# Value buffers as parts of one tile, wq in two transfers of three and two rows, and V of head 1 loaded ahead of K of head 2

## The chip, the cores and the metric

The kernel runs on one core of one Trainium2 chip. The metric is the device time of one execution in microseconds (us). A run more than 1.5% above the fastest of its kernel counts as slow.

The engines are PE (matrix products), DVE (vector), ACT (scalar), POOL, and SP, the sync engine, which in this kernel does nothing but issue loads. Sixteen DMA engines move the data. A load is issued once and is split over all sixteen. It has landed when the last of them is done. SP issues in program order: when the next load in its program has to wait for a buffer, every load behind it waits too. I call the loads that SP has issued and that haven't moved yet the **queue**.

## The reference, cut to what matters

```python
def reference(A_x, A_k_cache, A_v_cache, A_wq, A_wo, B_x, B_w1, B_w3, B_w2):
    # A_x [4, 1, 640]; caches [4, 32, 8192, 192]; wq [640, 6144]; all bf16
    xn = layernorm(A_x)
    q = (xn @ A_wq) as [4, 32 heads, 1, 192]
    k, v = the last W = 2048 rows of the caches
    p = softmax(einsum("bhqd,bhkd->bhqk", q, k) * 192 ** -0.5)
    attn = einsum("bhqk,bhkd->bhqd", p, v) as [4, 1, 6144] @ A_wo
    ffn = (silu(xn @ B_w1) * (xn @ B_w3)) @ B_w2          # F = 1536
    return A_x + attn + ffn
```

One decoding step reads 32 K tiles and 32 V tiles of 3.15 MB each (128 partitions of 24,576 B), wq of 7.86 MB, and smaller weights: 223 MB in all, for little arithmetic.

## The kernel before

All large loads go through the sync queue. K has two buffers and V has three. The query weights wq lie in the V buffers until the query projection has read them, so V of head 0 can't be loaded before that.

```python
kpool = tc.tile_pool(name="kt", bufs=KBUFS)      # KBUFS = 2
vpool = tc.tile_pool(name="vt", bufs=VBUFS)      # VBUFS = 3

def load_v(h):
    vt = (vpool if h < H - 1 else kpool).tile([P, NJ, Dh], BF16, ...)
    nc.sync.dma_start(out=vt..., in_=v_win[:, h]...)
    vts[h] = vt
# load_k(h) is the same with kpool and k_win
...
x_sb = const.tile([B, D], BF16, name="x_sb")
nc.scalar.dma_start(out=x_sb[:], in_=A_x...)     # x on ACT's queue
for k0 in range(0, KC, 2):                       # wq: 2 + 2 + 1 rows per partition
    n = min(2, KC - k0)
    wt = vpool.tile([P, 2, H * Dh], BF16, tag="vt")
    nc.sync.dma_start(out=wt[:, 0:n, :]..., in_=wq_v[:, k0:k0 + n, :]...)
for h in range(KBUFS):
    load_k(h)                                    # K of heads 0 and 1
...
xf = ppool.tile([B, D], FP32, tag="pr")
nc.vector.tensor_copy(out=xf[:], in_=x_sb[:])    # the x cast: start of LN, q projection, all heads
```

Each head is cut into four units u of a quarter tile. A unit has one DVE multiply of K by the query, an adder on PE (six matmuls that sum over the head dimension), and a DVE reduction. Four multiplies free a K buffer. Work is put into slots. A slot is emitted by phase, and this order is also the order on each engine.

```python
def mult(u):
    h, g = u // GQ, u % GQ                       # GQ = 4
    pr = ppool.tile([P, JQ, Dh], BF16, tag="pr")
    nc.vector.tensor_tensor(out=pr[:], in0=kts[h][:, g * JQ:(g + 1) * JQ, :], in1=<q of head h>, op=ALU.mult)
...
for h in range(H):
    u0, ul = h * GQ, h * GQ + GQ - 1
    if h >= KBUFS:
        add(*early.get(h, ((h - KBUFS + 1) * GQ, 0)), load_k, h)   # K(h): slot 4(h-1), waits for the multiplies on K(h-2)
    if h < H - 2:
        add(u0 + 2, 0, load_v, h)                                  # V(h): slot 4h+2
    for u in range(u0, ul + 1):
        add(u, 1, mult, u)
        add(u + 1, 2, adder, u)
        add(u + 1, 8, reduce_quarter, u)
...
add(3, 0, w1_load)                                                 # FFN weights in between
```

I write K2 for "K of head 2", and so on. In the sync queue the order is K0, K1, V0, w1, K2, V1, K3, V2, K4, V3 and so on. K2 waits until K0 has been multiplied, K4 until K2 has been multiplied.

## Time and profile before

| | before |
|---|---|
| median of 6 runs | 525.96 us (525.79 to 527.08) |
| span of the profiled execution (it took 525.93 us) | 524.1 us |
| bytes moved | 223.26 MB |

These lines are from the first parts of the profile page of the kernel before. The row "DMA" gives the busy tenths of the sixteen DMA engines in 40 equal slices of the span, the row "GB/s" what they moved. q1 is the queue of the large loads, q8 the queue on which instructions are fetched. The last line gives the shares of the chain of waits that ended last.

```profile
span 524.1 us, 4775 instructions
...
DMA  9999999999999999999999999999999999999996
GB/s 391 422 441 413 437 427 432 428 435 439 425 435 430 440 428 431 429 430 439 427 432 431 435 427 435 433 431 431 430 435 430 435 428 433 437 424 438 428 427 263
DMA packets 11138, 223.26 MB, mean 426 GB/s; under 512 B 1246, under 2 KB 1366, under 8 KB 1622
...
q1 hardware_dynamic: 11102, 222.96, 99.2%
q8 instruction: 15, 0.25, 0.2%
...
DMA 60%; DVE 19%; PE 18%; ACT 2%; issue 1%; SPq 0%
```

The DMA engines are at nine tenths or more in 39 of 40 slices. In stretches of 100 us and in one of 80, from 100 to 480 us, the window table gives 431 or 432 GB/s, and in stretches of 20 us 430 to 434. The Trainium skill ("DMA: Bandwidth & Descriptors", Where 436 GB/s comes from) works out a ceiling of 435.2 GB/s for the ports into the core's memory. This trace agrees: those long stretches lie within 1% of it. The same section says that for transfers between HBM, where the caches lie, and that memory a lower limit of about 358 GB/s binds. These loads come from HBM and run at 431 GB/s, so here the measurement decides. So the kernel is bound by DMA, and its time is the bytes divided by the rate, plus the moments at which an engine has no bytes to move.

The sync-queue timeline of the kernel before shows when loads were issued. Columns: start in us, length in us, SP's sequencer, source line, operation, destination and source, count.

```profile
25.96 0.54 SPq L134 DMA_DIRECT2D vt<-in_A_v_cache_dram  x1
...
40.58 0.54 SPq L128 DMA_DIRECT2D kt<-in_A_k_cache_dram  x1
...
42.19 0.57 SPq L134 DMA_DIRECT2D vt<-in_A_v_cache_dram  x1
51.86 0.54 SPq L128 DMA_DIRECT2D kt<-in_A_k_cache_dram  x1
...
65.00 0.54 SPq L128 DMA_DIRECT2D kt<-in_A_k_cache_dram  x1
65.63 0.55 SPq L134 DMA_DIRECT2D vt<-in_A_v_cache_dram  x1
```

The lines are V0, K2, V1, K3, K4 and V3. K2 was issued at 40.58, V1 right behind it, and K4 at 65.00.

The DVE timeline of the kernel before has the x cast and the first multiply on K2. The bracket gives DVE's idle time before it and what ended that.

```profile
6.89 0.48 DVE L180 CAST xf<-x_sb 4x640 f32<-4x640 bf16 x1 [4.01 <-DMA x_sb<-in_A_x_dram]
...
55.06 1.76 DVE L283 TENSOR_TENSOR pr<-kt,qbc 128x3072 bf16<-128x3072 bf16 x1 [2.63 <-DMA kt<-in_A_k_cache_dram]
```

x landed by 6.89 us, and K2 by 55.06 us. K4 was issued 65.00 - 55.06 = 9.9 us later, when K2's four multiplies were done.

### The profile page before, as it was taken

The page shows a single profiled execution, that of the slowest core. Times are in us where ns is not written, and L with a number is a line of the kernel's source. Part 1 is how long each engine was busy: PE and PEld are TensorE (multiplying, and loading weights), DVE is VectorE, ACT ScalarE, POOL GpSimd, SP SyncE. Part 2 cuts the span into 40 slices and gives each one's busy share as a digit, 9 for nine tenths or more (in the row PEclk, how much of TensorE's full clock was granted, in tenths as well). Part 3 has the DMA queues.
Part 4 walks back from the last instruction along what each step waited for, and adds up shares of the span by engine and source line. Part 5 has one row for each costly group of instructions (what it writes and reads, how often), then busy time and mean ns, then how long its engine had stood idle before and what let it go on. Part 6 is the DMA issues. An engine that isn't in the chain of part 4 may idle for free.

```text
span 524.1 us, 4775 instructions
## 1 busy us (share of the span) xinstructions
PE 356.9 (68%) x2327; PEld 75.5 (14%) x1633; DVE 339.3 (65%) x398; ACT 55.9 (11%) x176; POOL 5.4 (1%) x11
## 2 busy tenths in 40 slices
PE   0965867574685786863867676765776876685786
PEld 0100111110111111110111121111111111111122
DVE  3278756485676767763667876573776867666851
ACT  2111112000011101110110011100011110011020
POOL 4000000000000000000000000000000000000000
PEclk9989887977889988897898899888798898889898
DMA  9999999999999999999999999999999999999996
GB/s 391 422 441 413 437 427 432 428 435 439 425 435 430 440 428 431 429 430 439 427 432 431 435 427 435 433 431 431 430 435 430 435 428 433 437 424 438 428 427 263
DMA packets 11138, 223.26 MB, mean 426 GB/s; under 512 B 1246, under 2 KB 1366, under 8 KB 1622
## 3 DMA queue, kind: packets, MB, share of 16 engines
q1 hardware_dynamic: 11102, 222.96, 99.2%
q8 instruction: 15, 0.25, 0.2%
q14 instruction: 5, 0.04, 0.0%
q10 hardware_dynamic: 16, 0.01, 0.0%
HBM read 222.96 MB, written 0.01 MB: 425 GB/s over the span
## 4 chain that ended last, share of the span: by engine, by line
DMA 60%; DVE 19%; PE 18%; ACT 2%; issue 1%; SPq 0%
DMA kt<-in_A_k_cache_dram 52%; DVE pr L283 13%; PE ps L294 9%; DMA w<-in_B_w_dram 7%; PE po L367 3%; PE qps L248 3%; DVE sc L302 3%; DVE z L338 1%; DMA x_sb<-in_A_x_dram 1%; ACT ex L330 1%; PE acc L269 1%; PE mt L324 1%; ACT L330 0%; PE mt L311 0%; ACT negm L327 0%
## 5 line engine op out<-in xcount | busy, mean ns | idle before, releaser
L294 PE MATMUL ps<-pr,idb 128*128 128x512 bf16 x768 | 212.2, 418 | 145.9 <-DVE pr L283 145.8
L283 DVE TENSOR_TENSOR pr<-kt,qbc 128x3072 bf16<-128x3072 bf16 x128 | 223.5, 1747 | 106.6 <-DMA kt<-in_A_k_cache_dram 106.6
L302 DVE TENSOR_REDUCE sc<-ps 128x16 f32<-128x512 f32 x128 | 87.1, 681 | 1.5 <-PE ps L294 1.5
L346 PE MATMUL o_ps<-vt,z 128*8 128x384 bf16 x1024 | 55.5, 361 | 0.8 <-DMA vt<-in_A_v_cache_dram 0.8
L367 PE MATMUL po<-o_sb,sel_w 128*32 128x192 f32 x128 | 48.5, 513 | 1.1 <-ACT o_sb L349 1.1
L346 PEld LDWEIGHTS <-z 128*8 128x8 bf16 x1024 | 24.9, 92 | 101.4 <-issue 91.4
L338 DVE TENSOR_TENSOR z<-ex,mask_b 128x256 bf16<-128x256 bf16 x32 | 13.6, 425 | 34.1 <-ACT ex L330 34.0
L349 ACT COPY o_sb<-o_ps 128x384 f32<-128x384 f32 x32 | 15.3, 479 | 189.4 <-PE o_ps L346 189.4
L319 ACT ACTIVATE gneg<-gmax 1x128 f32<-1x128 f32 x32 | 9.8, 308 | 174.2 <-DVE gmax L316 174.2
L311 PEld LDWEIGHTS mt<-idf,lmax 128*1 128x1 f32 x32 | 3.3, 102 | 138.2 <-issue 138.2
L367 PEld LDWEIGHTS po<-o_sb,sel_w 128*32 128x32 f32 x128 | 14.2, 131 | 28.2 <-issue 24.7
L294 PEld LDWEIGHTS <-idb 128*128 128x128 bf16 x123 | 11.8, 96 | 37.4 <-issue 30.8
L324 PEld LDWEIGHTS mt<-ones_ff,gneg 1*128 1x128 f32 x64 | 9.4, 182 | 46.4 <-issue 39.2
L248 PE MATMUL qps<-wt,xnT 128*128 128x512 bf16 x59 | 14.7, 407 | 0.1
L316 DVE TENSOR_REDUCE gmax<-mt 1x4 f32<-1x128 f32 x32 | 8.8, 274 | 6.6 <-PE mt L311 6.5
L324 PE MATMUL mt<-ones_ff,gneg 1*128 1x1 f32 x64 | 12.1, 256 | 0.7 <-ACT gneg L319 0.7
L327 ACT COPY negm<-mt 128x1 f32<-128x1 f32 x32 | 5.1, 159 | 68.6 <-PE mt L324 68.6
L354 PEld LDWEIGHTS po<-rsum,tot_w 128*32 128x32 f32 x64 | 4.5, 108 | 49.3 <-ACT ex L330 35.3
L330 ACT ACTIVATE ex<-sc,negm 128x64 bf16<-128x64 f32 x32 | 11.1, 347 | 1.0
L254 DVE CAST qbc<-qps 128x512 bf16<-128x512 f32 x6 | 3.8, 685 | 11.5 <-PE qps L248 11.5
L311 PE MATMUL mt<-idf,lmax 128*1 128x128 f32 x32 | 11.1, 346 | 0.0
L202 PE MATMUL xnT_ps<-idb,xn 4*128 4x4 bf16 x5 | 0.4, 178 | 13.5 <-DVE xn L197 13.5
(73 smaller groups left out, 81.5 us busy)
## 6 DMA issues: line engine op xcount, KB each, us to landing
kt<-in_A_k_cache_dram SPq DMA_DIRECT2D x32, 3072.0 KB, 18.6
vt<-in_A_v_cache_dram SPq DMA_DIRECT2D x32, 3072.0 KB, 25.4
wt<-in_A_wq_dram SPq DMA_DIRECT2D x2, 3072.0 KB, 9.7
wo_t<-in_A_wo_dram SPq DMA_DIRECT2D x3, 1920.0 KB, 23.3
w<-in_B_w_dram SPq DMA_DIRECT2D x2, 1920.0 KB, 27.0
wt<-in_A_wq_dram SPq DMA_DIRECT2D x1, 1536.0 KB, 19.5
w<-in_B_w_dram SPq DMA_DIRECT2D x1, 1536.0 KB, 19.8
wo_t<-in_A_wo_dram SPq DMA_DIRECT2D x1, 1120.0 KB
```

The costliest lines, as they stand in the source:

```text
L248: nc.tensor.matmul(qp[:], lhsT=xnT[:, kc].rearrange("p a b -> p (a b)"), rhs=wq_rows[kc][:, (c0 + i) * QC:(c0 + i + 1) * QC], start=(kc == ...
L283: nc.vector.tensor_tensor(out=pr[:], in0=kts[h][:, g * JQ:(g + 1) * JQ, :], in1=qbc[:, h * Dh:(h + 1) * Dh].unsqueeze(1).to_broadcast([P, ...
L294: nc.tensor.matmul(ps[:], lhsT=idb[:], rhs=pr[:, :, kk * DD:(kk + 1) * DD], start=(kk == 0), stop=(kk == NK - 1))
L302: nc.vector.tensor_reduce(out=scs[h][:, g * JQ:(g + 1) * JQ], in_=pss.pop(u)[:], axis=AX.X, op=ALU.add)
L311: nc.tensor.transpose(out=mt[0:1, 0:P], in_=chs[h][0][:], identity=idf[:])
L319: nc.scalar.activation(out=gneg[:], in_=gmax[:].unsqueeze(1).to_broadcast([1, PB, B]), func=ACTF.Copy, scale=-SCALE)
L324: nc.tensor.matmul(mt[:, P:P + 1], lhsT=gneg[:].rearrange("o p b -> o (p b)"), rhs=ones_ff[:], start=True, stop=True)
L330: nc.scalar.activation(out=ex[:], in_=scs.pop(h)[:], func=ACTF.Exp, bias=negm[:, 0:1], scale=SCALE, accum_out=rsum[:])
L338: nc.vector.tensor_tensor(out=z[:], in0=ex[:].unsqueeze(2).to_broadcast([P, NJ, B]), in1=mask_b[:].unsqueeze(1).to_broadcast([P, NJ, B]), ...
L346: nc.tensor.matmul(o_ps[c * CT:c * CT + 2 * B, :], lhsT=z[:, 2 * jj:2 * jj + 2, :], rhs=vt[:, 2 * jj:2 * jj + 2, :], start=(jj < 4), stop= ...
L349: nc.scalar.copy(out=o_sb[:], in_=o_ps[:])
L367: nc.tensor.matmul(po_v[blk * CT:(blk + 1) * CT, :, x, :], lhsT=sel_w[:, par].rearrange("p a b -> p (a b)"), rhs=o_sb[:, par * Dh:(par + 1 ...
```

## The change

The change wants a freer hand in the V buffers and a fuller queue while the kernel starts. V1's buffer is free at about 29 us, as soon as wq has been read, but in the kernel before its load sits in the sync queue behind K2, which must wait for K0. Put ahead of K2, V1 is queued earlier. The V buffers become parts of one tile, so that wq can lie across them in 3 + 2 rows, with two transfers instead of three. The diff, cut (with "..." where lines are left out):

```diff
-    vpool = ctx.enter_context(tc.tile_pool(name="vt", bufs=VBUFS))
+    vpool = ctx.enter_context(tc.tile_pool(name="vt", bufs=1))
...
+    v_all = vpool.tile([P, VBUFS * NJ * Dh], BF16, name="v_all")
+    turn = [0]
+
+    def v_buffer():
+        i = turn[0] % VBUFS
+        turn[0] += 1
+        return v_all[:, i * NJ * Dh:(i + 1) * NJ * Dh].rearrange("q (j d) -> q j d", d=Dh)
...
     def load_v(h):
-        vt = (vpool if h < H - 1 else kpool).tile([P, NJ, Dh], BF16, ...)
+        vt = v_buffer() if h < H - 1 else k_buffer()
...
-    for k0 in range(0, KC, 2):
-        n = min(2, KC - k0)
-        wt = vpool.tile([P, 2, H * Dh], BF16, tag="vt")
-        nc.sync.dma_start(out=wt[:, 0:n, :].rearrange("p k n -> p (k n)"),
-                          in_=wq_v[:, k0:k0 + n, :].rearrange("p k n -> p (k n)"))
-        wq_rows += [wt[:, i, :] for i in range(n)]
+    wq_t = v_all[:, 0:KC * H * Dh].rearrange("p (k n) -> p k n", k=KC)
+    for k0, k1 in ((0, 3), (3, KC)):
+        nc.sync.dma_start(out=wq_t[:, k0:k1, :].rearrange("p k n -> p (k n)"),
+                          in_=wq_v[:, k0:k1, :].rearrange("p k n -> p (k n)"))
+    wq_rows = [wq_t[:, k, :] for k in range(KC)]
...
         if h < H - 2:
-            add(u0 + 2, 0, load_v, h)
+            add(*((u0 + 2, 0) if h != 1 else (KBUFS + 1, 0.5)), load_v, h)
```

On PE, DVE and ACT the instructions and their order are the same. On SP one transfer less is issued, and V1 moves.

More of the change, by code (lines that the diff above doesn't have):

```diff
@@ L99 @@
     assert (H * Dh) % QC == 0 and NQ % 6 == 0 and QW % P == 0 and Dh == RW * RPP and CT == HB * RW and P == FG * CT and F == FG * CT * FC
-    assert 2 * H * Dh <= NJ * Dh and KBUFS == 2 and VBUFS == 3 and HB * (Dh + 1) <= 512 and H // HG > 1
+    assert KC * H * Dh <= VBUFS * NJ * Dh and KC > 3 and KBUFS == 2 and VBUFS == 3 and HB * (Dh + 1) <= 512 and H // HG > 1
     nc.at_finalize(keep_loaded_weights)
@@ L124, with k_buffer @@
     wos, o_sbs, rsums, rts, chs, oTs = {}, {}, {}, {}, {}, {}
+    v_all = vpool.tile([P, VBUFS * NJ * Dh], BF16, name="v_all")
[4 more added lines that the diff above has]
+        return v_all[:, i * NJ * Dh:(i + 1) * NJ * Dh].rearrange("q (j d) -> q j d", d=Dh)
+    def k_buffer():
+        kt = kpool.tile([P, NJ, Dh], BF16, tag="kt", name="kt")
+        return kt[:]
     def load_k(h):
-        kt = (kpool if h < H - 1 else vpool).tile([P, NJ, Dh], BF16, tag="kt" if h < H - 1 else "vt", name="kt")
-        nc.sync.dma_start(out=kt[:].rearrange("q j d -> q (j d)"),
+        kt = k_buffer() if h < H - 1 else v_buffer()
+        nc.sync.dma_start(out=kt.rearrange("q j d -> q (j d)"),
                           in_=k_win[:, h].rearrange("b (p j) d -> p b (j d)", p=PB))
@@ L132, in load_v @@
     def load_v(h):
-        vt = (vpool if h < H - 1 else kpool).tile([P, NJ, Dh], BF16, tag="vt" if h < H - 1 else "kt", name="vt")
-        nc.sync.dma_start(out=vt[:].rearrange("q j d -> q (j d)"),
+        vt = v_buffer() if h < H - 1 else k_buffer()
+        nc.sync.dma_start(out=vt.rearrange("q j d -> q (j d)"),
                           in_=v_win[:, h].rearrange("b (p j) d -> p b (j d)", p=PB))
@@ L146 @@
     wq_v = A_wq.rearrange("(p kc) n -> p kc n", kc=KC)
-    wq_rows = []
-    for k0 in range(0, KC, 2):
-        n = min(2, KC - k0)
-        wt = vpool.tile([P, 2, H * Dh], BF16, tag="vt")
-        nc.sync.dma_start(out=wt[:, 0:n, :].rearrange("p k n -> p (k n)"),
-                          in_=wq_v[:, k0:k0 + n, :].rearrange("p k n -> p (k n)"))
-        wq_rows += [wt[:, i, :] for i in range(n)]
+    wq_t = v_all[:, 0:KC * H * Dh].rearrange("p (k n) -> p k n", k=KC)
[3 more added lines that the diff above has]
+    wq_rows = [wq_t[:, k, :] for k in range(KC)]
     for h in range(KBUFS):
```

## The prediction

> **What bounds it now.** The page's slice row shows the DMA engines at 9 tenths in 39 of 40 slices. 223 MB move in a 524.1 us span: 426 GB/s on average; the window table gives 431 to 434 GB/s in every long stretch from 60 to 480 us. The Trainium skill ("DMA: Bandwidth & Descriptors", Where 436 GB/s comes from) puts the ceiling of the 16 SBUF ports at 435.2 GB/s; this trace agrees, at most 1% below it. PE is busy 68%, DVE 65%. The chain of waits is 60% DMA. Only 0 to 8 us (348 GB/s) and 516 to 524 us (170 GB/s) are not full; at 432 GB/s they would save 1.6 and 4.8 us, mostly first latency and the closing matmuls and store.
>
> **What the change does.**
> - Bytes are unchanged. One DMA of 78 goes: one issue of about 0.4 us on the sync queue. Worth about 0.
> - The order view shows the same instructions on PE, DVE and ACT. On the sync queue only V of head 1 moves, ahead of K of head 2. Its waits stay by region, so the single tile costs no wait on the whole buffer.
> - wq 3+2: rows 0 to 2 land about 13.4 us (2 rows took 9.7 us, one more row is 3.6 us at 432 GB/s), before xnT lets PE start at 15.09. Row 3 now comes with row 4, which landed near 20.8 us; PE reached row 3 at 20.17. So PE waits about 0.6 us once; no DMA waits for that while the queue is full.
> - V of head 1 was issued at 42.19 us, behind K of head 2 (40.58, waiting for the multiplies on head 0). It now goes at about 28.5 to 29.5. Was the queue about to run dry? Issued by 40 us: 19.1 MB; moved by then (window table): 16.7 MB. So 2.4 MB, 5.5 us, were still queued when K of head 2 came: no gap to close; the cushion just grows to about 13 us.
> - The price: K of head 2 lands one tile (3.15 MB, 7.3 us) later, about 62.3 instead of 55.06 us. Its multiplies take about 9.9 us (55.06 to 65.0), so K of head 4 is issued about 72 instead of 65 us. Bytes issued before that last until about 76 us, so the queue thins to roughly 4 us but should not run dry. K of head 3 and later tiles land as before: by then the same bytes precede them.
>
> **On the critical path:** nearly nothing: same bytes, rate, first DMA and tail. I allow -0.5 us (thin spots at 40 to 54 us, where 419 GB/s was measured) to +1 us (a short gap near 74 to 77 us).
>
> **Prediction:** 525.8 us, range 524.5 to 527.5; faster by over 2%: 0.01, within 2%: 0.98, slower by over 2%: 0.01.
>
> **What would show it.** The DMA rate from 60 to 480 us stays 431 to 434 GB/s; sync-queue timeline: V of head 1 at about 29 us, K of head 2 about 41, K of head 4 about 72; DVE waits until about 62 us for K of head 2; K of head 3 still near 70 us and K of head 4 near 85.6; PE waits about 0.6 us for wq; w2 lands near 516 us as before.
>
> **What would make it wrong.** A real gap in the queue before 54 us that the averages hide (up to 1 us faster); a DMA gap near 76 us, which shifts all that follows; 36 KB rows per partition moving slower or faster than 24 KB ones; a changed reuse of completion semaphores that makes a later load wait. None reaches 2% (10.5 us).

## The result, and the profile after

| | before | after |
|---|---|---|
| median of 6 runs | 525.96 us (525.79 to 527.08) | 528.02 us (527.14 to 529.53) |
| profiled execution | 525.93 us, span 524.1 us | 527.32 us, span 525.5 us |
| ratio of fast runs | 1 | 1.0038, 95% interval 1.0017 to 1.0058 |

A ratio here is the mean time of one kernel's fast runs over the mean of the other's fast runs of the same rounds, so it isn't quite the ratio of the medians. The change costs 0.4%, and the median lies 0.5 us above the predicted range. The profiled execution after is one of the quicker ones of its kernel: it shows 1.4 us of the median's 2.1 us.

From the page of the kernel after:

```profile
span 525.5 us, 4775 instructions
...
DMA  9999999999999999999999999999999999999996
GB/s 382 427 441 408 429 401 428 429 442 427 438 428 434 431 427 436 427 436 432 431 435 428 434 431 427 436 428 438 428 434 432 430 436 428 432 430 430 438 425 261
```

The span is 1.4 us longer at the same bytes. The largest drop among the early slices is in the sixth (65.7 to 78.8 us): it has 401 GB/s, where before had 427 (65.5 to 78.6 us). From the seventh slice on, both rows scatter around the same 431.

The sync-queue timeline of the kernel after:

```profile
28.99 0.54 SPq L147 DMA_DIRECT2D v_all<-in_A_v_cache_dram  x1
...
31.58 0.54 SPq L147 DMA_DIRECT2D v_all<-in_A_v_cache_dram  x1
44.24 0.54 SPq L141 DMA_DIRECT2D kt<-in_A_k_cache_dram  x1
...
55.51 0.56 SPq L141 DMA_DIRECT2D kt<-in_A_k_cache_dram  x1
...
74.98 0.54 SPq L141 DMA_DIRECT2D kt<-in_A_k_cache_dram  x1
75.61 0.56 SPq L147 DMA_DIRECT2D v_all<-in_A_v_cache_dram  x1
```

The lines are V0, V1, K2, K3, K4 and V3. V1 is queued at 31.58, as intended. K4 is queued at 74.98 instead of 65.00, ten us later.

The DVE timeline of the kernel after:

```profile
8.44 0.48 DVE L191 CAST xf<-x_sb 4x640 f32<-4x640 bf16 x1 [5.56 <-DMA x_sb<-in_A_x_dram]
...
63.19 1.76 DVE L294 TENSOR_TENSOR pr<-kt,qbc 128x3072 bf16<-128x3072 bf16 x1 [7.10 <-DMA kt<-in_A_k_cache_dram]
```

K2 landed at 63.19 us, 8.1 us later than before: it lies behind one more tile of 3.15 MB. DVE waited 7.10 us for it instead of 2.63. Also, x came 1.55 us later (8.44 against 6.89).

The two stretches of the window table that matter follow, first of the kernel before, then of the kernel after. Columns: window in us, its length, busy time (and instructions) of PE, PE's weight loads, DVE, ACT and POOL, the granted TensorE clock (1.00 is full speed), the mean busy share of the DMA engines, GB/s. A packet counts as a whole in the window in which it starts, so a share can lie above 1.

```profile
74.00:76.00 2.00, 2.00 (x13) 0.73 (x12) 2.00 (x4) 1.46 (x2) 0.00 (x0) 0.50 0.97 418
76.00:78.00 2.00, 2.00 (x29) 0.54 (x25) 0.75 (x1) 0.62 (x2) 0.00 (x0) 1.00 1.08 467
78.00:80.00 2.00, 2.00 (x11) 0.39 (x3) 0.00 (x0) 0.89 (x2) 0.00 (x0) 1.00 1.00 430
```

```profile
74.00:76.00 2.00, 0.99 (x5) 0.00 (x0) 2.00 (x3) 0.00 (x0) 0.00 (x0) 1.00 0.69 295
76.00:78.00 2.00, 2.00 (x36) 0.79 (x33) 1.97 (x4) 0.08 (x1) 0.00 (x0) 1.00 1.07 381
78.00:80.00 2.00, 2.00 (x16) 0.38 (x11) 2.00 (x4) 0.43 (x2) 0.00 (x0) 1.00 0.97 418
```

Between 74 and 78 us the rate fell to 295 and 381 GB/s, where before had 418 and 467. That is the gap. In the packet records of the trace (not shown on the page; a packet is one row of a load, here 24 KB, on one DMA engine) the number of DMA engines with a packet in flight falls from 16 at 75.25 us to 5 at 76.25 and is back at 16 at 77.25. K4 was issued at 74.98, and its first bytes moved 1.3 us after that. So the load came just too late: the engines ran dry one after another while it was still being started.

The same pieces of work took longer as well. The PE timelines of both kernels, before first, show the first adder of K2, six matmuls that use the same instructions in both:

```profile
56.87 1.46 PE L294 MATMUL ps<-pr,idb 128*128 128x512 bf16 x6 [0.50 <-DVE pr L283]
```

```profile
65.00 2.72 PE L305 MATMUL ps<-pr,idb 128*128 128x512 bf16 x6 [5.13 <-DVE pr L294]
```

They took 1.46 us before and 2.72 us after. The granted TensorE clock was 1.0 in the one case and 0.5 in the other (in the kernel after it was 0.5 from 63.5 to 70.3 us). The slower PE reaches DVE through the softmax of head 1. DVE works in program order, and two steps of that softmax stand between K2's multiplies: a maximum (gmax), which needs PE, and z, which needs ACT and before that PE. The DVE timelines, before first, show the waits:

```profile
59.26 0.27 DVE L316 TENSOR_REDUCE gmax<-mt 1x4 f32<-1x128 f32 x1
62.28 0.42 DVE L338 TENSOR_TENSOR z<-ex,mask_b 128x256 bf16<-128x256 bf16 x1 [0.49 <-ACT ex L330]
```

```profile
67.97 0.28 DVE L327 TENSOR_REDUCE gmax<-mt 1x4 f32<-1x128 f32 x1 [0.50 <-PE mt L322]
72.26 0.43 DVE L349 TENSOR_TENSOR z<-ex,mask_b 128x256 bf16<-128x256 bf16 x1 [1.75 <-ACT ex L341]
```

DVE waited 2.25 us instead of 0.49. That is nearly the whole difference between K2's four multiplies after, 74.98 - 63.19 = 11.8 us, and before, 9.9 us.

### Where the time of a run ends

The trace holds one landing per DMA engine for each load. The last load is the last piece of wo. In 17 profiles, the time of the profiled execution was the mean landing of that load over the sixteen engines, plus the lag of the slowest engine behind the mean, plus 5.0 us (5.00 to 5.17). The 17 are all profiles but that of e12, whose execution was a slow one. This splits a run's cost into bytes that came late on all engines and one engine that fell behind. Each number below comes from the profiled execution; "empty" is engine time without any packet, divided by 16 engines.

| kernel | profiled us | mean landing | lag of the slowest | empty at 42 to 52 us | empty at 74 to 90 us |
|---|---|---|---|---|---|
| before | 525.93 | 519.66 | 1.10 | none | 0.01 |
| after | 527.32 | 521.05 | 1.26 | none | 0.57 |
| after again (e4) | 528.89 | 521.73 | 2.17 | none | 1.02 |
| order only (e1) | 528.49 | 520.67 | 2.71 | none | 0.62 |
| tile and wq only (e2) | 526.85 | 520.24 | 1.60 | 0.15 | 0.01 |
| tile only (e3) | 526.03 | 519.82 | 1.10 | – | – |
| V1 and V2 ahead (e5) | 533.95 | 527.25 | 1.69 | – | 7.00 |
| half of V1 ahead (e6) | 526.34 | 520.04 | 1.21 | none | 0.00 |
| V3 ahead of K4 (e7) | 526.50 | 520.17 | 1.32 | – | 0.01 |
| DVE late, 7 casts (e9) | 528.08 | 521.53 | 1.41 | 1.50 | – |
| DVE late, 13 casts (e10) | 529.94 | 523.51 | 1.33 | 3.34 | – |

In the profile of after, 1.39 us of mean landing are to be explained. 0.57 us are empty engines at 74 to 90 us. Another 0.40 us are packets that were slower than the usual 912 ns for 24 KB just after the engines started again. Some 0.15 to 0.2 us were already lost in the first loads. That leaves about 0.2 us spread over the rest.

### The profile page after: what moved, and what is told of

Same layout as the page of the kernel before. It is cut to its first block, busy times and chain, and to the rows that moved or that the text cites. A ratio compares the mean times of both kernels' runs of the same rounds, so it can differ in the third digit from the quotient of the medians.

```text
span 525.5 us, 4775 instructions
## 1 busy us (share of the span) xinstructions
PE 358.2 (68%) x2328; PEld 75.7 (14%) x1633; DVE 338.9 (64%) x398; ACT 55.9 (11%) x176; POOL 5.5 (1%) x11
## 4 chain that ended last, share of the span: by engine, by line
DMA 60%; DVE 19%; PE 18%; ACT 2%; issue 1%; SPq 0%
DMA kt<-in_A_k_cache_dram 52%; DVE pr L294 12%; PE ps L305 9%; DMA w<-in_B_w_dram 7%; PE po L378 3%; PE qps L259 3%; DVE sc L313 3%; DMA x_sb<-in_A_x_dram 1%; DVE z L349 1%; ACT ex L341 1%; PE acc L280 1%; PE mt L335 1%; PE o_ps L357 1%; ACT negm L338 0%; PE mt L322 0%
## 5 line engine op out<-in xcount | busy, mean ns | idle before, releaser
L294 DVE TENSOR_TENSOR pr<-kt,qbc 128x3072 bf16<-128x3072 bf16 x124 | 216.6, 1747 | 103.5 <-DMA kt<-in_A_k_cache_dram 103.5
L357 PE MATMUL o_ps<-v_all,z 128*8 128x384 bf16 x992 | 54.8, 366 | 0.4 <-DMA v_all<-in_A_v_cache_dram 0.4
L305 PEld LDWEIGHTS <-idb 128*128 128x128 bf16 x123 | 11.9, 97 | 37.8 <-issue 31.2
L259 PE MATMUL qps<-v_all,xnT 128*128 128x512 bf16 x60 | 16.2, 437 | 0.0
L335 PE MATMUL mt<-ones_ff,gneg 1*128 1x1 f32 x64 | 12.1, 256 | 0.7 <-ACT gneg L330 0.7
```

Source lines behind the costliest of these rows:

```text
L259: nc.tensor.matmul(qp[:], lhsT=xnT[:, kc].rearrange("p a b -> p (a b)"), rhs=wq_rows[kc][:, (c0 + i) * QC:(c0 + i + 1) * QC], start=(kc == ...
L305: nc.tensor.matmul(ps[:], lhsT=idb[:], rhs=pr[:, :, kk * DD:(kk + 1) * DD], start=(kk == 0), stop=(kk == NK - 1))
L335: nc.tensor.matmul(mt[:, P:P + 1], lhsT=gneg[:].rearrange("o p b -> o (p b)"), rhs=ones_ff[:], start=True, stop=True)
L357: nc.tensor.matmul(o_ps[c * CT:c * CT + 2 * B, :], lhsT=z[:, 2 * jj:2 * jj + 2, :], rhs=vt[:, 2 * jj:2 * jj + 2, :], start=(jj < 4), stop= ...
```

## The experiments

Sixteen runs were made, in four rounds: ten new kernels, the kernel after once more (e4), and e2's kernel five more times (e11, e13 to e16). The theories are named by letters in the texts, which were written before each run. In short:

- **Q**: V1 ahead delays K2, and through K2's multiplies K4, so the queue is empty near 76 us.
- **W**: the 3 + 2 wq transfers cost time of their own at the start, apart from the order.
- **T**, a rival of both: the single tile makes loads wait longer for their buffers.
- **S** came later: the tile with 3 + 2 rows makes x, q and so K2's issue late, and the queue is nearly empty before K2 comes.
- **P**, its rival: the larger wq packets cost something by themselves.
- **L**, in round 4: one DMA engine falls behind the others and stays behind.

### Round 1: the parts of the change

**e1, the order alone**, on the kernel before:

```diff
-            add(u0 + 2, 0, load_v, h)
+            add(*((u0 + 2, 0) if h != 1 else (KBUFS + 1, 0.5)), load_v, h)
```

> The kernel before with only V of head 1 moved ahead of K of head 2 (separate tiles, wq 2+2+1). Theory Q (the DMA queue runs dry because K of head 2 lands one tile later and K of head 4, which waits for its multiplies, is issued about 10 us later than before): K of head 2 lands at 62 to 63 us, K of head 4 is issued at 72 to 75 us, DMA below 350 GB/s for one or two us near 76 us, time 526.8 to 528 us. Theory W (the 3+2 split of wq starts the kernel worse): no loss, 526 us. Theory T (the shared tile): no loss, 526 us.

Measured: 528.33 us (526.5 to 532.18), ratio 1.0049 (1.0023 to 1.0075). From its sync-queue timeline (V1, K2, K4) and its window table:

```profile
29.57 0.55 SPq L134 DMA_DIRECT2D vt<-in_A_v_cache_dram  x1
42.53 0.53 SPq L128 DMA_DIRECT2D kt<-in_A_k_cache_dram  x1
...
74.23 0.54 SPq L128 DMA_DIRECT2D kt<-in_A_k_cache_dram  x1
```

```profile
74.00:76.00 2.00, 1.74 (x5) 0.00 (x0) 2.00 (x3) 0.00 (x0) 0.00 (x0) 0.62 0.80 320
```

K2 landed at 62.9, K4 was issued at 74.23, and the rate at 74 to 76 us fell to 320 GB/s. Theory Q's chain is all there without the tile and without the wq split, and the cost is of the size of the whole change. The time is 0.3 us above the range that Q expected.

**e2, the tile and wq 3 + 2, the old order**, on the kernel after:

```diff
-            add(*((u0 + 2, 0) if h != 1 else (KBUFS + 1, 0.5)), load_v, h)
+            add(u0 + 2, 0, load_v, h)
```

> The changed kernel with V of head 1 back in its old place (shared tile and wq 3+2 kept). Theory Q: x lands and the q projection ends 1.5 to 3 us later as in the changed kernel, but no gap near 76 us and 525.8 to 526.5 us. Theory W: the slow start costs as much as in the changed kernel, 527.5 to 528.5 us. Theory T: the same.

Measured: five fast runs of 526.85 to 530.32 us (median 527.88) and one slow one of 545.01; ratio of fast runs 1.0043 (1.0024 to 1.0063). From its sync-queue timeline (K2, K4):

```profile
43.66 0.55 SPq L141 DMA_DIRECT2D kt<-in_A_k_cache_dram  x1
...
67.47 0.54 SPq L141 DMA_DIRECT2D kt<-in_A_k_cache_dram  x1
```

K4 is issued at 67.47, in time, and the trace has no gap at 76 us. Still the kernel is slower and its times are spread widely. That isn't what Q alone expects. e3, next, differs from this kernel in the wq transfers alone, so these have a cost of their own, as W said.

**e3, the tile alone**, on the kernel after, with wq in 2 + 2 + 1 rows and the old order:

```diff
-    for k0, k1 in ((0, 3), (3, KC)):
+    for k0, k1 in ((0, 2), (2, 4), (4, KC)):
...
-            add(*((u0 + 2, 0) if h != 1 else (KBUFS + 1, 0.5)), load_v, h)
+            add(u0 + 2, 0, load_v, h)
```

> Only the shared tile: wq in 2+2+1 and V of head 1 in its old place. Theories Q and W: 526 us, x lands at 6.9 us as before. Theory T: slower by 1 us or more.

Measured: 526.03 us (525.66 to 527.11), ratio 1.0006 (0.9992 to 1.002). x came at 7.09 us. No cost of the single tile is seen, and T falls.

**e4, the kernel after once more**, in the same rounds:

> The changed kernel again, for a ratio from the same rounds and a second profile. Theory Q: 527 to 529.5 us; the gap near 76 us is there again, and its length moves with the time at which K of head 4 is issued. If the gap is a chance of the first profile, it is missing here at an unchanged time.

Measured: 528.39 us (527.13 to 530.43), ratio 1.0046 (1.0027 to 1.0065). The order costs 0.49%, tile and wq cost 0.43%, both together 0.46%: the two don't add. A reason that fits is that e2's weak spot lies before K2, near 46 us, and V1 ahead of K2 fills just that spot; the packet records show no empty engines at 42 to 52 us in e1, e4 and after, and 0.15 us in e2. The price moves to 76 us.

### Round 2: more of the suspected cause, and less of it

**e5, V1 and V2 ahead of K2**, twice the dose, on the kernel after:

```diff
-            add(*((u0 + 2, 0) if h != 1 else (KBUFS + 1, 0.5)), load_v, h)
+            add(*((u0 + 2, 0) if h not in (1, 2) else (KBUFS + 1, 0.5)), load_v, h)
```

> The changed kernel with V of head 2 ahead of K of head 2 as well: double the suspected cost. Theory Q (the queue empties near 76 us because K of head 4 waits for the multiplies on a late K of head 2): K of head 2 lands about 70 us, its multiplies end and K of head 4 is issued about 80 to 82 us, nothing moves from about 76 to 82 us, time 531 to 535 us. Rival (the loss in the changed kernel comes from the slow start alone or from chance engine lags): 527 to 529 us as in the changed kernel.

Measured: 535.63 us (533.95 to 537.06), ratio 1.019 (1.0174 to 1.0206). K4 in the sync-queue timeline, and the window table:

```profile
81.43 0.55 SPq L141 DMA_DIRECT2D kt<-in_A_k_cache_dram  x1
```

```profile
74.00:76.00 2.00, 2.00 (x7) 0.52 (x5) 1.50 (x4) 0.31 (x1) 0.00 (x0) 0.80 0.66 283
76.00:78.00 2.00, 2.00 (x10) 0.45 (x4) 1.44 (x1) 0.00 (x0) 0.00 (x0) 1.00 0.19 80
78.00:80.00 2.00, 1.56 (x9) 0.27 (x4) 1.29 (x3) 0.60 (x3) 0.00 (x0) 1.00 0.00 0
80.00:82.00 2.00, 0.55 (x2) 0.00 (x0) 2.00 (x3) 0.00 (x0) 0.00 (x0) 0.90 0.00 0
```

K2 landed at 70.1 and K4 was issued at 81.43. The DMA engines stood still from 78 to 82 us, 7.00 us of empty time per engine in all, and the profiled execution was 8.0 us longer than that of before. This settles the mechanism: each tile put ahead of K2 delays K4 by about a tile (10.0 us for the first, 6.5 us for the second; a tile takes 7.3 us), and once the queue is used up, the delay is paid in full: against the profile of after, K4 came 6.5 us later and the execution took 6.6 us more. The median lies 0.6 us above the range that Q expected. This trace also shows what a start costs: from K4's issue to its first packet 1.32 us passed (81.43 to 82.75), and eight of the engines began at 82.75 to 82.89 us, the other eight at 83.56 to 83.82.

**e6, half of V1 ahead**, the other half at the old place; wq 3 + 2 and the tile kept:

```diff
+    def load_v_half(h, i): ...                   # half the columns of each partition
...
-        if h < H - 2:
-            add(*((u0 + 2, 0) if h != 1 else (KBUFS + 1, 0.5)), load_v, h)
+        if h == 1:
+            add(KBUFS + 1, 0.5, load_v_half, h, 0)
+            add(u0 + 2, 0, load_v_half, h, 1)
+        elif h < H - 2:
+            add(u0 + 2, 0, load_v, h)
```

> The changed kernel with only the first half of V of head 1 ahead of K of head 2, the second half behind it: half the suspected cost. Theory Q: K of head 2 lands about 59.5 us, K of head 4 is issued about 70 to 71.5 us, 4 us before the queue is empty; no gap near 76 us and, as the half tile covers 46 us too, none there: 525.9 to 526.8 us. Rival (order is not the cause): 527 to 529 us.

Measured: 526.34 us (526.25 to 527.33), ratio 1.0008 (0.9996 to 1.002). K4's line in the sync-queue timeline:

```profile
71.41 0.54 SPq L141 DMA_DIRECT2D kt<-in_A_k_cache_dram  x1
```

K2 landed at 59.5, K4 was issued at 71.41, and neither spot is empty. K2's multiplies took 71.41 - 59.50 = 11.9 us here. Against e2, half of V1 ahead takes back nearly all of the cost; against after, so does leaving the other half behind.

**e7, V3 ahead of K4**, on the kernel after. V3's buffer is free before K2's multiplies are done:

```diff
-            add(*((u0 + 2, 0) if h != 1 else (KBUFS + 1, 0.5)), load_v, h)
+            add(*((u0 + 2, 0) if h not in (1, 3) else ((KBUFS + 1, 0.5) if h == 1 else (u0, -1))), load_v, h)
```

> The changed kernel with V of head 3, whose buffer is free by about 60 us, ahead of K of head 4 on the in-order sync queue: K of head 4 stays as late, but there is something to move. Theory Q: V of head 3 is issued about 58 to 60 us, K of head 4 still about 75 us, no gap near 76 us, 526 to 527 us. Rival (a late K of head 4 costs by itself, or the start does): 527 to 529 us as in the changed kernel.

Measured: 526.50 us (526.22 to 527.24), ratio 1.001 (0.9998 to 1.0022). The sync-queue timeline (V2 and V3 in one line, then K4) and the window table:

```profile
56.83 3.62 SPq L147 DMA_DIRECT2D v_all<-in_A_v_cache_dram  x2
74.57 0.53 SPq L141 DMA_DIRECT2D kt<-in_A_k_cache_dram  x1
```

```profile
74.00:76.00 2.00, 1.41 (x10) 0.02 (x7) 2.00 (x3) 0.00 (x0) 0.00 (x0) 1.00 1.06 455
```

K4 is as late as in after (74.57 against 74.98), but the rate at 74 to 76 us is 455 GB/s instead of 295, since V3 was in the queue from about 59.9 us on (the end of that line: 56.83 + 3.62 = 60.45, less its own issue of about half a us). So it isn't the lateness of K4 that costs, but the empty queue: with V3 in it, the time is back within 0.1% of before's (the interval reaches 0.2%). In after V3 had to stand behind K4 until 75.61. The Trainium skill ("DMA: Bandwidth & Descriptors", Anatomy of one DMA) says that DMA engines do not wait on semaphores; the wait happens on the sequencer that issues. The two traces agree: a buffer free at 59.9 us was filled only when the sequencer got to it.

**e8, x loaded before the start barrier, with the tile and wq 3 + 2 in the old order.** The edit to e2's kernel lets the function that moves SP's first load ahead of the barrier do the same for ACT's, which is x:

```diff
-        sp = mybir.EngineType.SP
-        i, ins = next(...)
-        ...
+        for sp in (mybir.EngineType.SP, mybir.EngineType.Activation):
+            i, ins = next(...)
+            ...
```

> Shared tile and wq 3+2 with V of head 1 in its old place (as the run of tile and wq that took 528.5 us), and the load of x issued before the start barrier, 0.8 us earlier, ahead of most wq packets. Theory S (wq 3+2 costs because x, held up behind 36 KB packets, makes the q projection, and so K of head 2, 3 us late, when the queue is nearly empty at 46 us): x lands before 5 us, K of head 2 is issued 1 to 2.5 us earlier than the 43.7 us measured there, and the time falls to 525.8 to 526.8 us with a narrow range. Theory P (36 KB packets or the engine lags that they start with cost by themselves): stays at 527.5 to 529 us and wide.

Measured: 526.89 us (525.97 to 529.97), ratio 1.0021 (1.0 to 1.0041). x came at 5.65 us instead of 8.43, and K2 was issued at 41.93 instead of 43.66. K2 gained less than x, since PE now had to wait 1.6 us for the second wq transfer (at 21.1 us). The ratio halved, with intervals that overlap, and the times stayed wide. It lies between the expectations of S and P and tells nothing certain.

### Round 3: the start made late on purpose

**e9 and e10, the kernel before with the x cast repeated**, 7 and 13 times. The repeats write the same value, so the result stays right; they only make DVE late, with the old wq and the old order. In e9 it reads range(7), in e10 range(13):

```diff
-    nc.vector.tensor_copy(out=xf[:], in_=x_sb[:])
+    for _ in range(7):
+        nc.vector.tensor_copy(out=xf[:], in_=x_sb[:])
```

> The kernel before with its first copy of x repeated seven times on DVE: the q projection starts about 2.9 us later, transfers untouched (separate tiles, wq 2+2+1, old order). Theory S (a late head alone makes K of head 2 late, when the queue is nearly empty at 46 us): K of head 2 is issued about 43.5 us, and the time is 526.5 to 529 us with a wide range, as with wq 3+2. Theory P (36 KB packets cost by themselves): 526 us and narrow, as before.

Measured: 527.17 us (526.55 to 528.08), ratio 1.0015 (0.9994 to 1.0036; one of before's runs in this round took 529.7). K2 was issued at 45.95, not at the 43.5 that I had expected. In the profile, which fell on the slowest of the six runs, 1.50 us per engine were empty.

> The same with thirteen copies, about 5.8 us: K of head 2 is issued about 46.4 us, after the last queued byte has moved. Theory S: a plain gap of 1.5 to 3 us near 46 to 48 us, time 528 to 531 us. Theory P: 526 us.

Measured: 530.42 us (528.88 to 530.64), ratio 1.0069 (1.0045 to 1.0093). K2 in the sync-queue timeline, and the window table:

```profile
47.97 0.54 SPq L128 DMA_DIRECT2D kt<-in_A_k_cache_dram  x1
```

```profile
46.00:48.00 2.00, 1.04 (x6) 0.00 (x0) 2.00 (x3) 0.00 (x0) 0.00 (x0) 1.00 0.11 41
48.00:50.00 2.00, 1.45 (x6) 0.00 (x0) 2.00 (x2) 0.00 (x0) 0.00 (x0) 1.00 0.53 132
50.00:52.00 2.00, 1.56 (x7) 0.18 (x2) 1.97 (x4) 0.00 (x0) 0.00 (x0) 1.00 0.81 344
```

3.34 us per engine were empty, and the profiled execution took 3.9 us more than the median of before on the same chip (529.94 against 526.06). K2 was issued at 47.97, not at 46.4 as expected. So an empty queue before K2 is paid for too, as much as one before K4. It was large with K2 at 45.95 and 47.97; e2's kernel, with K2 at 43.66, isn't there.

**e11, e2's kernel again, one look:**

> Shared tile and wq 3+2 without the reordering once more, for a second profile, as its first profile fell on its fastest run (526.85 of a median of 528.5). Theory S: a run slower than 527.5 us shows K of head 2 issued at 44 us or later and a rate below 350 GB/s near 46 to 48 us. If such a run shows no gap there, the loss in slow runs comes from somewhere else.

Measured: 526.10 us in a single run, K2 issued at 43.68, no gap. It fell on a quick run and tells nothing.

**e12, a candidate that might beat both**: the kernel before (wq 2 + 2 + 1) with x early, as in e8, and half of V1 ahead, as in e6.

> The kernel before (separate tiles, wq 2+2+1) with x loaded before the start barrier and the first half of V of head 1 ahead of K of head 2: cushions on both sides. Theory Q with S: no gap at 46 or 76 us; the mean of the 16 engines cannot end earlier than in the kernel before, so 525.5 to 526.2 us, at most the occasional run of 527 us goes away. It would have to be under 525.6 us to beat the kernel before.

Measured: 526.08 us, six fast runs of 525.97 to 526.17; the profiled run, 534.7, was a slow one. The ratio is 0.9993 (0.9971 to 1.0015). It doesn't beat the kernel before. As the DMA engines of before are not empty at either spot (42 to 52 and 74 to 90 us), there is nothing there for an earlier load to fill.

### Round 4: what a slow run of e2's kernel looks like

The prediction was wrong and one thing was still open: why e2's kernel has runs of 527.5 to 530.3 us (all of them fast) although its profile shows nearly no empty engine. The four runs are looks at the same kernel, with no edit to it, to catch a slow one in a profile.

> Shared tile and wq 3+2 in the old order, a third profile. Theory S: if it takes over 527.3 us, K of head 2 is issued after 44.5 us and the rate falls under 350 GB/s for at least a us between 45 and 49 us. Theory L (engine lags): no gap, but the slowest engine ends over 2 us behind the mean of the 16.

> The same once more. Theory S: over 527.3 us only with K of head 2 issued after 44.5 us and a gap near 46 us. Theory L: no gap, slowest engine over 2 us behind the mean.

> The same once more. Theory S: over 527.3 us only with K of head 2 issued after 44.5 us and a gap near 46 us. Theory L: no gap, slowest engine over 2 us behind the mean.

> The same once more. Theory S: over 527.3 us only with K of head 2 issued after 44.5 us and a gap near 46 us. Theory L: no gap, slowest engine over 2 us behind the mean.

Measured, each a single run of unknown state, beside 525.89 us of before on the same chip:

| look | us | mean landing | lag of the slowest | K2 issued | empty at 42 to 52 us |
|---|---|---|---|---|---|
| e13 | 528.33 | 521.36 | 1.94 | 43.88 | 0.18 |
| e14 | 530.20 | 523.94 | 1.23 | 43.62 | 0.05 |
| e15 | 528.50 | 520.90 | 2.60 | 44.06 | 0.24 |
| e16 | 527.34 | 520.59 | 1.75 | 43.92 | 0.28 |
| before | 525.93 | 519.66 | 1.10 | 40.58 | none |

By their letter both theories fail. All four runs took over 527.3 us with K2 issued before 44.5 us, against S, and only in e15 did one engine end over 2 us behind the mean, as L asks. In three of the four (e13, e15, e16) some engines were empty for a moment before K2's packets came, and one engine ended 1.75 to 2.6 us behind the mean, where in before it is 1.1. But empty engines are the smaller part. e14 shows the larger one most clearly. These are the window tables of e14 and of before over the same 28 us:

```profile
56.00:84.00 28.00, 22.70 (x158) 4.87 (x119) 16.77 (x18) 5.22 (x11) 0.00 (x0) 0.84 1.01 390
```

```profile
56.00:84.00 28.00, 18.61 (x137) 4.09 (x90) 18.70 (x22) 5.83 (x13) 0.00 (x0) 0.92 1.00 431
```

The engines are equally busy (1.01 and 1.00), but they moved 390 GB/s instead of 431. A 24 KB packet took 1.02 us instead of 0.912 on all sixteen engines, from about 48 to 84 us. 28 us at 41 GB/s less are 1.15 MB, or 2.7 us at 431 GB/s. This is most of the 4.3 us by which e14's mean landing is later than before's, and no load was late. The other three have such packets too, e13 for about 10 us (388 GB/s from 48 to 58 us, against 426 in before), e15 and e16 for a few us. Summed over the packet records of 44 to 90 us, packets slower than 912 ns cost 1.2, 3.9, 0.7 and 0.4 us per engine more in e13 to e16 than in before, and empty engines 0.05 to 0.28 us.

So S explains only a small part of these runs. Nor is the slow stretch bound to the 3 + 2 rows: the trace of e12's slow run, with wq in 2 + 2 + 1 rows, has it as well (1.02 to 1.05 us for most packets from 50 to 124 us, 379 GB/s from 52 to 80 us). The looks show what these runs lose, not that the wq transfers cause it. Why the packets of such a run are slow, and why one engine falls behind and stays behind, remains open.

## Why the prediction was wrong

The class, within 2%, was right. The time was not: 528.02 us against 525.8, and above the range's end of 527.5.

**What held.** The same bytes moved at the same rate in the long middle (431 to 433 GB/s from 100 to 480 us after, in stretches of 20 us). The single tile costs no waits (e3, ratio 1.0006). V1 was issued at 31.58 us (29 predicted). K2 landed one tile later, at 63.19 (62.3 predicted). The place of a possible gap, 74 to 77 us, was named as a risk.

**The step that failed** is this one: "K of head 4 is issued about 72 instead of 65 us. Bytes issued before that last until about 76 us, so the queue thins to roughly 4 us but should not run dry." The chain was right, and the terms of the sum were each a little too small:

| term | predicted | measured in after |
|---|---|---|
| K2 lands | 62.3 us | 63.19 us |
| four multiplies on K2 | 9.9 us | 11.8 us |
| K4 is issued | 72 us | 74.98 us |
| from issue to first packet | not counted | 1.3 us |
| the queue lasts until | 76 us | 75.25 us for the first engine, 2 to 3 us later for the last |

Predicted 4 us to spare became about 75.25 - 74.98 - 1.3 = -1.0 us for the quickest engine. The multiplies were the largest mis-sized term. I took their length from one head of one profile, K2 of before, where PE ran at full clock. Over all eighteen profiles K2's multiplies took 9.9 to 12.1 us. They took 9.9 us only in the three (before, e8, e15) in which a granted clock of 0.5 covered less than 1 us of them, and 10.7 us or more where it covered 1.5 us or more. The same trace of before had a warning: K3's four multiplies ran from 70.02 to 83.73, 13.7 us. That is no like case, though, since FFN matmuls ran on PE between them.

**That engines run dry one by one was not seen.** I counted the queue as one pool of bytes. In after the first engine was out of packets at 75.25 us, while others had work for another 2 us. The Trainium skill ("DMA: Bandwidth & Descriptors", Two DMAs through the same engine are not ordered) says that nothing orders DMAs across the 16 engines; in e5, the engines went from 16 busy at 75.2 us to none at 78.2 us, which agrees. After the gap they don't start evenly either. In e1 one engine and in e4 two had their next packet only at 78.2 to 78.7 us, some 2 us after the others, and these packets took 1.9 to 2.2 us instead of 0.912. The slowest engine ended 2.71 and 2.17 us behind the mean, against 1.10 in before and 1.26 in the profile of after. A run's time follows the slowest engine, so this lag is paid on top.

**wq was mis-sized in another way.** I predicted 0.6 us of waiting on PE for row 3. PE did not wait: in after it came to row 3 at 23.42 us, and the second transfer had landed by 21.13. What came instead was x itself, 0.6 to 1.6 us later wherever wq went in packets of 36 KB and x in its old place (7.7 to 8.4 us, against 6.9 to 7.1 with 24 KB). x runs on another queue than wq and has to pass the same sixteen engines. The Trainium skill ("DMA: Bandwidth & Descriptors", Queues, rings and completion order) says that an engine alternates between queues at packet granularity. That a small load therefore waits for a large packet to end is my inference: the page's packet is a group of descriptors, which need not be what the profile calls a packet, and no run varied packet size alone, so it isn't shown.

A later x makes the query projection, K0's multiplies and so K2's issue later, but it is less than half of the matter. In after K2 was issued 3.66 us later than in before: 1.55 us from x, 1.48 us because the query projection itself took longer (16.20 against 14.72 us), and 0.63 us because K0's multiplies did. The projection had no waits; its matmuls were slow for longer. Six matmuls took 2.5 us at first and 1.3 us later, and the clock records of full speed begin at 18.0 us in before and at 22.5 us in after. So K2's issue varies from profile to profile. With 3 + 2 rows it came at 44.24 (after), 43.66 (e2), 42.59 (e4) and 40.89 (e6). With 2 + 2 + 1 rows it came at 42.53 (e1), 42.26 (e3) and 40.58 (before). The one profile on which I based the prediction is the earliest of all in which x was loaded in its old place.

**The cushion of 5.5 us before K2 was too large for the same reasons.** The term takes K2's issue of the one early profile. With K2 at 42.3 to 44 us and 1.3 us for the start, about 0.8 to 2.5 us are left by the same count, and for the engine that is ahead nothing is left at times, as e13 to e16 show.

**What the order cost and what the wq cost don't add:** 0.49% and 0.43% alone, 0.46% together. That V1 ahead of K2 keeps the queue full when K2 comes late fits this, but isn't shown to be the reason.

**What stays open:** why the wq transfers in 3 + 2 rows cost what they do (e2 against e3: 0.43% against 0.06%), why packets are slow for tens of us in some runs (e13, e14, and e12's slow run), and why an engine that was empty for a moment then loses one us or more.

## What to carry to other kernels

Moving load A ahead of load B in an in-order queue delays B, what is computed from B, and the load that B's buffer is reused for: count the queue at that later load, not only at the spot that A fills. Count it in time, subtract the start of a load (1.3 us here), take the quickest of the engines, and take the compute time that the slower clock gives, not the one at hand. Here a cushion of -1.0 us was paid for, and about -0.5 us in e1. In e6 the same count leaves about 75.25 - 71.41 - 1.3 = 2.5 us (an estimate), and next to nothing was lost. No run lies between. Where the cushion is short, put something free in between (e7), or move only a half (e6): both took the cost back, to 0.1% (intervals up to 0.2%).

## What the Trainium skill lacked or had wrong

- "DMA: Bandwidth & Descriptors", Latency and other measured facts, gives about 600 ns to the first byte for a load issued by sync or scalar. From the start of the issuing instruction to the first packet these traces show 1.32 us (e5), 1.32 us (e10) and 1.34 us (e9), of which 0.54 us are the instruction itself. The page doesn't say from when it counts; from the end of the instruction it was about 0.8 us. The last engine started 0.8 to 1.1 us after the first. The page has no figure for that.
- The same page, Two DMAs through the same engine are not ordered, has no word on what it costs in time: the engines were up to 3 us apart (e5, 75.2 to 78.2 us), the lag of one stayed to the end (1.05 to 2.7 us behind the mean), and the run's time was 5.0 to 5.2 us more than the landing of the slowest in all 17 profiles.
- "Runtime: NRT & Kernel Launch", Instruction fetch mechanics, calls the cost of crossing a 16 KiB boundary "mostly hidden". In a kernel bound by DMA the fetch takes DMA time: the 15 fetches of before (q8, 16,384 B each, 0.88 to 1.04 us) are counted among the packets of the same sixteen engines, and within 0.02 us of the end of 13 of them a 24 KB packet started that took 1.38 to 1.46 us instead of 0.91. Whether a compute engine waited for one was not looked at.
- No page has stretches in which every packet is slower: 1.02 us instead of 0.912 us for 24 KB, for 36 us, with full queues (e14), and 1.02 to 1.05 us in e12's slow run.
- No page gives the time of the first packets after an empty queue: 1.2 to 1.6 us for most engines of after, and up to 2.2 us (e1, e4), instead of 0.912 us.
- "DMA: Bandwidth & Descriptors", Where 436 GB/s comes from, has about 358 GB/s as the limit that binds for transfers between HBM and the core's memory: this kernel loaded from HBM at 431 GB/s for hundreds of us.
